# A half unit of w_out products moved inside the fourth visit of each frame

## Chip, cores, metric

The kernel runs on one core of one Trainium2 chip. The metric is device time in microseconds (us) of one execution; three executions of the kernel before took 860.3, 860.36 and 861.01 us, median 860.36.

Engines go by short names: PE is the tensor engine's matmuls, PEld its weight loads, DVE the vector engine, ACT the scalar engine, SP the engine that issues the transfers.

## The reference

An attention over q, k, v (4 batches, 8 heads, 576 positions, 64 wide; four heads see the last 32 positions, four see every 32nd) gives 2304 rows of 512. Two MLPs of the same shape follow, both with weights that come in as inputs:

```
def _moe_ref(x, w_in, w_out):       # x 2304x512, w_in 512x2048, w_out 2048x512
    h = x @ w_in
    r = np.maximum(h, 0.0)
    g = r * r
    return (g @ w_out)

def _moe2_ref(x, w_in, w_out):      # on the result of the first
    h = np.maximum(x @ w_in, 0.0)
    return (h * h @ w_out)
```

## The kernel before

The order of all work is written out by hand (the program is built under a manual schedule), and each engine runs its own instructions in that order. Engines wait for one another by semaphores.

Attention, the first MLP and one narrow block of the second take the first 549 us or so. The rest is the second MLP on four blocks of 512 tokens, and the change lies there. Both products of a block are done by a seven-product scheme (sums and differences of 256-wide quarters, seven products in place of eight). Every operand is split into a high and a low part, so one product is three matmuls: high by high, high by low, low by high.

A block k has eight pairs q of hidden slices. The function `seven` goes over the 32 (k, q) and calls `frame` for all but the last, so 31 times. One call, a frame, does the first product (by w_in) of the next pair and, in between, the second product (by w_out) of this pair:

- The first product is four **visits** (`visit`). The first has 12 matmuls (products "11" and "s2"), the second 6 ("12"), the third 12 ("s1", "s3"), the fourth 12 ("s4", "22"). All four write the same PSUM bank: the pool `ps_h` has one buffer, tile `ps_m`. So the first matmul of each visit waits until the visit before it has been read out.
- The second product is seven **units** of two halves (`n_unit`), 14 half units of 3 matmuls each into other banks (`ps_y`). `seven` deals them into four `gaps`, one behind each visit.

Every one of the 84 matmuls of a frame is 128x128 by 128x256 with a weight load of its own. I call one load with its matmul a **step**. So a frame is, on the tensor engine: first visit 12 steps, `gaps[0]` 9, second visit 6, `gaps[1]` 9, third visit 12, `gaps[2]` 15, fourth visit 12, `gaps[3]` 9.

What the vector engine does around the change, in its order:

```
        add(u..., ps..., u2...)      # reads all of the third visit's bank: u<-ps_m 128x512
        add(a22, ps[:, :HT], u3)     # reads it again: r<-ps_m 128x256
        ...
        each(gaps[2])
        each(late)
        rest(bh[:, 1], bl[:, 1], a22)
        visit(k, q, ps, ("s4", 5), ("22", 6))
        add(of["c"], ps, u)          # reads the fourth visit's bank: c<-ps_m 128x512
```

The fourth visit's first matmul waits for the second of these adds. The next frame's first visit waits for the third, `c<-ps_m`.

In the profile's line numbers of the kernel before, a visit's matmuls are L1279, a half unit's L1306 and the adds L1112. In the first frame of a block (q = 0) the output of the block before is summed and stored as well, so the scalar and vector engines have more to do there. I call the three such frames of which a block precedes (the 9th, 17th and 25th) boundary frames, and the others plain.

Of the kernel before, what the change touches and what calls it, by code (L numbers as in the profile page):

```python
# [169 lines left out]
def tile_attention_then_two_mlps(  # L170
# [218 lines left out]
    def tt(out, in0, in1, op):  # L389
        nc.vector.tensor_tensor(out=out, in0=in0, in1=in1, op=op)  # L390
# [48 lines left out]
    for i in range(0, half2, 2):  # L439
        n = i + 2 if i + 2 < half2 else None  # L440
# [656 lines left out]
    def each(todo):  # L1097
        for one in todo:
            one()

    def high(hi, src):
        nc.scalar.activation(out=hi, in_=src, func=AF.Copy)  # L1102

    def rest(hi, lo, src):
        tt(lo, src, r32(hi), ALU.subtract)
# [5 lines left out]
    def add(dst, src, to, sign=1.0):  # L1111
        nc.vector.scalar_tensor_tensor(  # L1112
            out=dst, in0=src, scalar=sign * W_BACK, in1=to, op0=ALU.mult, op1=ALU.add
        )
# [83 lines left out]
    def x_op(k, i):  # L1198
        at = (k - NB) % 2 * 10 + 2 * i if i < 5 else 10 + 2 * i
        return [  # L1200
            xall[:, 48 + (at + a) * TB:48 + (at + a + 1) * TB].rearrange("p (c n) -> p c n", c=2)
            for a in range(2)
        ]

    def load_x(k, half):
        t0, n = BLOCKS[1][k - NB]
        for c in (2 * half, 2 * half + 1):
            nc.sync.dma_start(out=others[:, c * TB:(c + 1) * TB], in_=y_dram[:, c, t0:t0 + n])
# [30 lines left out]
    pairs7 = [(k, q) for k in range(NB + 1, 2 * NB) for q in range(NF // 2)]  # L1239
# [27 lines left out]
    def m_weights(q, name):  # L1267
        if name[0] == "s":
            return [t[:, int(name[1]) - 1] for t in s_parts[NF + 2 * q]]
        w = wt["in", 1, 2 * q + int(name[0]) - 1]  # L1270
        return [w[:, int(name[1]) - 1, a] for a in range(2)]

    def visit(k, q, ps, *products):
        for half, (name, i) in enumerate(products):
            w_hi, w_lo = m_weights(q, name)
            x_hi, x_lo = x_op(k, i)
            for j in range(2):
                for m, (w, x) in enumerate(((w_hi, x_hi), (w_hi, x_lo), (w_lo, x_hi))):
                    nc.tensor.matmul(  # L1279
                        ps[:, half * HT:(half + 1) * HT],  # L1280
                        lhsT=w[:, j * P:(j + 1) * P],
                        rhs=x[:, j],
                        start=half == 0 and j == 0 and m == 0,
                        stop=half + 1 == len(products) and j == 1 and m == 2,
                    )

    def squares(t):
        nc.vector.scalar_tensor_tensor(out=t, in0=t, scalar=0.0, in1=t, op0=ALU.max, op1=ALU.mult)  # L1288
# [26 lines left out]

        return [lambda t=t: half(t) for t in range(2)]

    def frame(gaps, nxt, cur, copies=((), (), ()), end=False, x=((), (), ()), late=()):

        k, q = nxt  # L1320
        if not of:
            of["r"] = gpool.tile([P, TB], F32, tag="r", name="r", bufs=1)
            of["c"] = gpool.tile([P, TB], F32, tag="sq", name="c", bufs=1)
            shapes = {"bh": ("qk0", 4), "bl": ("qk1", 4), "ah": ("qk2", 3)}
            for t, (tag, n) in shapes.items():
                of[t] = fpool.tile([P, n * HALF], F32R, tag=tag, name=t, bufs=1).rearrange(
                    "p (i n) -> p i n", i=n)
            for t, n in (("al", 2), ("al2", 1)):
                of[t] = gpool.tile([P, 3 * HALF], F32R, tag="gl", name=t, bufs=2)[
                    :, 48:48 + n * HALF].rearrange("p (i n) -> p i n", i=n)  # L1330
        r, c = (of[t].rearrange("p (h n) -> p h n", h=2) for t in ("r", "c"))
        a11, a22, a21, a12 = r[:, 0], r[:, 1], c[:, 0], c[:, 1]
        ah, al, bh, bl = (of[t] for t in ("ah", "al", "bh", "bl"))
        sums_x, high_x, rest_x = x

        def positive(t, src):
            nc.scalar.activation(out=t, in_=src, func=AF.Relu)
            nc.scalar.activation(out=t, in_=t, func=AF.Square)

        if cur:  # L1340
            s13, s24 = (
                gpool.tile([P, TB + P], F32, tag="gh", name="s", bufs=2)[:, :TB].rearrange(
                    "p (i n) -> p i n", i=2)
                for _ in range(2)
            )
            high(ah[:, 2], a12)
            tt(s13[:, 0], a21, a22, ALU.add)
            tt(s13[:, 1], a11, a21, ALU.subtract)
            rest(ah[:, 2], of["al2"][:, 0], a12)
            tt(s24[:, 0], s13[:, 0], a11, ALU.subtract)  # L1350
            tt(s24[:, 1], a12, s24[:, 0], ALU.subtract)
        each(copies[0])
        ps = ps_h.tile([P, TB], F32, tag="h", name="ps_m")
        visit(k, q, ps, ("11", 0), ("s2", 1))
        m, u = (vpool.tile([P, 512], F32, tag="val", name="u") for _ in range(2))

        c11, u2 = m[:, :HT], m[:, HT:]
        u3 = u[:, HT:]
        nc.scalar.activation(out=m, in_=ps, func=AF.Copy, scale=W_BACK)  # L1359
        tt(u2, c11, u2, ALU.add)  # L1360
        each(copies[1])
        if cur:
            high(ah[:, 0:2], s13)
            high(bh[:, 2:4], s24)
        each(copies[2])
        each(gaps[0])
        if end:
            first_sum()
            rest(ah[:, 0:2], al, s13)
        visit(k, q, ps, ("12", 2))  # L1370
        add(c11, ps[:, :HT], c11)
        if cur:
            rest(bh[:, 2:4], bl[:, 2:4], s24)
        if cur and not end:
            rest(ah[:, 0:2], al, s13)
        each(sums_x)
        if end:
            each(high_x)
            each(rest_x)
        positive(a11, c11)  # L1380
        high(bh[:, 0], a11)
        if not end:
            each(high_x)
        each(gaps[1])
        if nxt == pairs7[0]:
            ps = ps_a.tile([P, TB], F32, tag="a", name="ps_m")
        visit(k, q, ps, ("s1", 3), ("s3", 4))
        add(
            u.rearrange("p (h n) -> p h n", h=2),
            ps.rearrange("p (h n) -> p h n", h=2),  # L1390
            u2.unsqueeze(1).to_broadcast([P, 2, HT]),
        )
        add(a22, ps[:, :HT], u3)
        positive(a22, a22)
        high(bh[:, 1], a22)
        rest(bh[:, 0], bl[:, 0], a11)
        if not end:
            each(rest_x)
        each(gaps[2])
        each(late)  # L1400
        rest(bh[:, 1], bl[:, 1], a22)
        visit(k, q, ps, ("s4", 5), ("22", 6))
        add(of["c"], ps, u)
        squares(of["c"])
        each(gaps[3])
# [4 lines left out]
    def first_sum():  # L1410
        acc["p1"] = tile_of("pt")
        nc.scalar.activation(out=acc["p1"], in_=banks["11"], func=AF.Copy, scale=W_BACK)

    def sums_late(last):
        acc["u"], acc["o12"], acc["o"] = tile_of("pt"), tile_of("s"), tile_of("s")
        add(acc["u"], banks["s2t2"], acc["p1"])
        if last:
            add(acc["o12"], banks["s1t1"], acc["u"])
# [99 lines left out]
    def seven():  # L1518
        copies, sums = None, []
        for n, (k, q) in enumerate(pairs7[:-1]):  # L1520
            todo = [one for name in ORDER for one in n_unit(k, q, name)]
            gaps = todo[:3], todo[3:6], todo[6:11], todo[11:]
            end = q == NF // 2 - 1 or n + 2 == len(pairs7)
            more = k < last7
            x = [[], [], []]
            if more and q == 0:
                x_work[k + 1] = x_works(k + 1)
            if more and q > 1:
                x = [list(part) for part in x_work[k + 1][q - 2]]
            late = [lambda: sums_late(not more)] if end else []  # L1530
            if sums:
                first, then = sums.pop(0)
                x[0] += first
                late += then
            frame(gaps, pairs7[n + 1], True, copies or ((), (), ()), end, x, late)
            copies = None
            if more and q in (1, 2):
                load_x(k + 1, q - 1)
            if end and more:
                copies, sums = sums_then(k)  # L1540
        finish()
# [8 lines left out]
    with tc.manual_schedule():  # L1550
# [3 lines left out]
        ps = ps_h.tile([P, TB], F32, tag="h", name="ps_w")[:, :P]  # L1554
# [19 lines left out]
        for s in range(len(steps)):  # L1574
            k, f = steps[s]
            layer, j = blocks[k]
# [41 lines left out]
            if k == NB - 1:  # L1618
                load2("in")
        seven()  # L1620

# [36 lines left out]
```

## Time and profile before

| | us |
|---|---|
| median of three runs | 860.36 (860.3 to 861.01) |
| the profiled execution's own time | 860.37 |
| its span, first to last instruction | 858.6 |
| so around the span | 1.77 |
| PE busy | 847.8 (99%) |
| PEld busy | 770.4 (90%) |
| DVE busy | 681.2 (79%) |
| ACT busy | 526.3 (61%) |

The profile is of one execution. Its own time is within 0.01 us of the median. Busy shares are over all stages. A matmul's busy time is counted from its start to its modelled end, and neighbours overlap, so the distance from one weight load's start to the next says more about pace than the busy time does.

### The profile page before, as it was taken

Reading aid. Unit: us, or ns where it says so; the run is one execution under the profiler, and the core shown is the slowest. Engines: PE = TensorE matmul, PEld = TensorE weight load, DVE = VectorE, ACT = ScalarE, POOL = GpSimd, SP = SyncE. Lnnn points to the kernel's source line nnn. Section 1 sums busy time; section 2 is a strip of 40 time slices with the busy share of each in tenths; the row PEclk is TensorE's granted clock in tenths of the full one; section 3 lists DMA queues with packets and bytes.
Section 4 is the critical chain, followed back from the end, with each engine's and each line's share of the span. In section 5 each row is a group of like instructions: output and inputs, shape, how many; then the busy total and the mean of one; then the engine's idle time right before and its main releaser. Section 6 shows DMA issues by size and latency. Waiting matters only on the chain. (4 is left out here: it accounts for less than half of the span.)

```text
span 858.6 us, 16041 instructions
## 1 busy us (share of the span) xinstructions
PE 847.8 (99%) x5719; PEld 770.4 (90%) x5719; DVE 681.2 (79%) x1710; ACT 526.3 (61%) x1216; POOL 16.8 (2%) x15
## 2 busy tenths in 40 slices
PE   8899999999999999999999999999999999999998
PEld 8778888888788888899888899999999999999998
DVE  5899895489775777478889996678888888888877
ACT  6987775467675666376666774555555564556442
POOL 0610000000000000000000000000000000000000
PEclk9999999999999999999999999999999999999999
DMA  8964721222222221268996476476668667766764
GB/s 268 336 218 160 238 64 45 89 77 76 73 78 97 62 71 59 74 244 296 344 364 211 155 269 233 133 226 202 193 197 282 188 192 238 244 188 197 230 186 133
DMA packets 82399, 155.21 MB, mean 181 GB/s; under 512 B 7568, under 2 KB 36368, under 8 KB 80272
## 3 DMA queue, kind: packets, MB, share of 16 engines
q1 hardware_dynamic: 82320, 154.19, 55.0%
q8 instruction: 45, 0.74, 0.3%
q14 instruction: 34, 0.28, 0.1%
HBM read 127.95 MB, written 26.21 MB: 180 GB/s over the span
## 5 line engine op out<-in xcount | busy, mean ns | idle before, releaser
L975 PE MATMUL ps_h<-xall,w 128*128 128x512 f32 (+1 forms) x1153 | 247.2, 358 | 0.0
L975 PEld LDWEIGHTS ps_h<-xall,w 128*128 128x128 f32 x1153 | 185.1, 188 | 25.9
L975 PE MATMUL ps_y<-gh,w 128*128 128x512 f32 (+1 forms) x640 | 155.8, 374 | 0.7 <-ACT gh L1024 0.7
L975 PEld LDWEIGHTS ps_y<-gh,w 128*128 128x128 f32 x640 | 107.9, 188 | 17.6 <-ACT gh L1024 1.1
L1279 PE MATMUL ps_m<-xall,s 128*128 128x256 f32 x768 | 104.5, 279 | 0.3 <-DVE r L1112 0.3
L1018 ACT ACTIVATE r<-ps_h 128x512 f32<-128x512 f32 x80 | 47.7, 597 | 87.2 <-PE ps_h L975 78.2
L1279 PEld LDWEIGHTS ps_m<-xall,s 128*128 128x128 f32 x768 | 95.5, 188 | 0.9 <-DVE r L1112 0.8
L1306 PE MATMUL ps_y<-w,bh 128*128 128x256 f32 x496 | 91.8, 278 | 0.0
L975 PE MATMUL ps_y<-gl,w 128*128 128x512 f32 (+1 forms) x324 | 83.8, 370 | 0.0
L1279 PE MATMUL ps_m<-xall,w 128*128 128x256 f32 x576 | 83.3, 280 | 0.0
L1306 PEld LDWEIGHTS ps_y<-w,bh 128*128 128x128 f32 x496 | 75.3, 188 | 0.0
L1279 PEld LDWEIGHTS ps_m<-xall,w 128*128 128x128 f32 x576 | 74.2, 188 | 0.4 <-ACT u L1359 0.4
L1029 DVE TENSOR_TENSOR gl<-sq,gh 128x512 fp32r<-128x512 f32 x80 | 55.3, 691 | 21.7 <-ACT gh L1024 17.1
L1306 PE MATMUL ps_y<-w,ah 128*128 128x256 f32 x372 | 70.1, 278 | 0.0
L1306 PE MATMUL ps_y<-w,bl 128*128 128x256 f32 x248 | 68.8, 277 | 0.0
L1027 DVE TENSOR_TENSOR sq<-r 128x512 f32<-128x512 f32 x38 | 26.3, 692 | 50.7 <-ACT r L1018 50.7
L975 PEld LDWEIGHTS ps_y<-gl,w 128*128 128x128 f32 x324 | 55.7, 188 | 9.6 <-DVE gl L1029 0.4
L1306 PEld LDWEIGHTS ps_y<-w,ah 128*128 128x128 f32 x372 | 56.7, 189 | 0.0
L1112 DVE SCALAR_TENSOR_TENSOR u<-ps_m,u 128x256 f32<-128x256 f32 x64 | 35.7, 558 | 25.4 <-PE ps_m L1279 25.3
L680 ACT ACTIVATE s<-s,m 96x128 f32<-96x128 f32 (+2 forms) x88 | 34.3, 390 | 33.6 <-DVE m L564 32.9
L1102 ACT ACTIVATE ah<-c 128x256 fp32r<-128x256 f32 x33 | 13.7, 418 | 63.6 <-DVE c L1288 63.6
L1306 PE MATMUL ps_y<-w,al 128*128 128x256 f32 x186 | 51.7, 278 | 0.0
(121 smaller groups left out, 1500.7 us busy)
## 6 DMA issues: line engine op xcount, KB each, us to landing
w<-w_mem SPq DMA_DIRECT2D x221, 256.0 KB, 2.8
raw<-moe_w_in_d SPq DMA_DIRECT2D x32, 512.0 KB, 5.8
raw<-moe_w_out_d SPq DMA_DIRECT2D x24, 512.0 KB, 5.1
w_mem<-xall SPq DMA_DIRECT2D x16, 512.0 KB, 4.2
w_mem<-xall SPq DMA_DIRECT2D x8, 1024.0 KB, 5.3
xall<-w_mem SPq DMA_DIRECT2D x8, 1024.0 KB, 5.5
qk<-loc_qk_d SPq DMA_DIRECT2D x12, 416.0 KB, 3.1
out_d<-o SPq DMA_DIRECT2D x17, 256.0 KB, 2.4
```

The source lines that it names most:

```text
L680: nc.scalar.activation(out=blk, in_=blk, func=AF.Exp, scale=-1.0, bias=m[:nq, j:j + 1], accum_out=dens[i][:nq, j:j + 1],)
L975: nc.tensor.matmul(y[:, c:c + w], lhsT=lhsT, rhs=rhs[:, c:c + w], start=start and c == 0, stop=stop and c + w == n,)
L1018: nc.scalar.activation(out=r, in_=ps, func=AF.Relu, scale=W_BACK)
L1027: nc.vector.tensor_tensor(out=sq, in0=r, in1=r, op=ALU.mult)
L1029: nc.vector.tensor_tensor(out=lo, in0=sq, in1=r32(h), op=ALU.subtract)
L1102: nc.scalar.activation(out=hi, in_=src, func=AF.Copy)
L1112: nc.vector.scalar_tensor_tensor(out=dst, in0=src, scalar=sign * W_BACK, in1=to, op0=ALU.mult, op1=ALU.add)
L1279: nc.tensor.matmul(ps[:, half * HT:(half + 1) * HT], lhsT=w[:, j * P:(j + 1) * P], rhs=x[:, j], start=half == 0 and j == 0 and m == 0, sto ...
L1306: nc.tensor.matmul(banks[name][:, t * HALF:(t + 1) * HALF], lhsT=g[:, rows], rhs=w, start=first and t == 0 and m == 0, stop=end and t == 1 ...
```

## The change

`visit` gets an argument `between`, work that is issued after its first matmul. `frame` hands one through to its fourth visit. `seven` gives `gaps[2]` four half units in place of five, and the fifth (number 10 of 14, the first half of unit "s3t3") goes in as `between`. The frame that stands in the narrow block calls without it.

```
-    def visit(k, q, ps, *products):
+    def visit(k, q, ps, *products, between=None):
         for half, (name, i) in enumerate(products):
...
                 for m, (w, x) in enumerate(((w_hi, x_hi), (w_hi, x_lo), (w_lo, x_hi))):
+                    if half == 0 and j == 0 and m == 1 and between is not None:
+                        between()
                     nc.tensor.matmul(
...
-        visit(k, q, ps, ("s4", 5), ("22", 6))
+        visit(k, q, ps, ("s4", 5), ("22", 6), between=between)
...
-            gaps = todo[:3], todo[3:6], todo[6:11], todo[11:]
+            gaps = todo[:3], todo[3:6], todo[6:10], todo[11:]
...
-            frame(gaps, pairs7[n + 1], True, copies or ((), (), ()), end, x, late)
+            frame(gaps, pairs7[n + 1], True, copies or ((), (), ()), end, x, late, todo[10])
```

On the tensor engine, from the last but one half unit of `gaps[2]` to the end of the fourth visit of a plain frame, before (`ah` and `al` are the two parts of a hidden operand, `w` the ring of w_out, `xall` and `s` or `w` the visit's operands):

```order
L1306 MATMUL ps_y<-w,ah 128x256 [waits DMAHW2_49]
L1306 MATMUL ps_y<-w,ah 128x256
L1306 MATMUL ps_y<-w,al 128x256 [waits DVE_49]
L1306 MATMUL ps_y<-w,ah 128x256 x2
L1306 MATMUL ps_y<-w,al 128x256
L1306 MATMUL ps_y<-w,ah 128x256 [waits DMAHW3_49]
L1306 MATMUL ps_y<-w,ah 128x256
L1306 MATMUL ps_y<-w,al 128x256
L1279 MATMUL ps_m<-xall,s 128x256 [waits DVE_49]
L1279 MATMUL ps_m<-xall,s 128x256 x5
L1279 MATMUL ps_m<-xall,w 128x256 x6
```

The same place of the changed program:

```order
L1308 MATMUL ps_y<-w,ah 128x256 [waits DMAHW2_49]
L1308 MATMUL ps_y<-w,ah 128x256
L1308 MATMUL ps_y<-w,al 128x256 [waits DVE_49]
L1308 MATMUL ps_y<-w,ah 128x256 x2
L1308 MATMUL ps_y<-w,al 128x256
L1281 MATMUL ps_m<-xall,s 128x256 [waits DVE_49]
L1308 MATMUL ps_y<-w,ah 128x256 [waits DMAHW3_49]
L1308 MATMUL ps_y<-w,ah 128x256
L1308 MATMUL ps_y<-w,al 128x256
L1281 MATMUL ps_m<-xall,s 128x256 x5
L1281 MATMUL ps_m<-xall,w 128x256 x6
```

The visit's first matmul, with its wait for the vector engine, now stands three matmuls earlier, and the half unit with its wait for a transfer stands behind it.

On the same engine in the first boundary frame, around the same place, before:

```order
L1306 MATMUL ps_y<-w,ah 128x256 x2
L1306 MATMUL ps_y<-w,al 128x256
L1306 MATMUL ps_y<-w,ah 128x256 [waits DMAHW0_49,PE_49,Activation_49]
L1306 MATMUL ps_y<-w,ah 128x256
L1306 MATMUL ps_y<-w,al 128x256
L1279 MATMUL ps_m<-xall,s 128x256 [waits DVE_49]
L1279 MATMUL ps_m<-xall,s 128x256 x5
```

And in the changed program:

```order
L1308 MATMUL ps_y<-w,ah 128x256 x2
L1308 MATMUL ps_y<-w,al 128x256
L1281 MATMUL ps_m<-xall,s 128x256 [waits DVE_49]
L1308 MATMUL ps_y<-w,ah 128x256 [waits DMAHW0_49,PE_49,Activation_49]
L1308 MATMUL ps_y<-w,ah 128x256
L1308 MATMUL ps_y<-w,al 128x256
L1281 MATMUL ps_m<-xall,s 128x256 x5
```

There too the same three rows have changed places with the visit's first. All other rows of the tensor engine, and all rows of the other engines and their waits, are the same but for line numbers.

## Rows read from the trace of the kernel before

**Rows 1.** Page, engines: busy us, share of the span, instructions.
```profile
PE 847.8 (99%) x5719; PEld 770.4 (90%) x5719; DVE 681.2 (79%) x1710; ACT 526.3 (61%) x1216; POOL 16.8 (2%) x15
```

**Rows 2.** Windows, one plain and one boundary frame; columns named in the first row.
```profile
core 0: us, PE busy (x) PEld busy (x) DVE busy (x) ACT busy (x) POOL busy (x), PEclk, DMA share, GB/s
646.76:656.49 9.72, 9.72 (x87) 9.72 (x85) 8.29 (x18) 5.20 (x12) 0.00 (x0) 1.00 0.86 293
...
705.09:714.86 9.77, 9.77 (x87) 9.75 (x85) 8.21 (x18) 5.91 (x14) 0.00 (x0) 1.00 0.65 181
```

**Rows 3.** Instructions of tile ps_m from 549 us on: count, ns min/median/max.
```profile
L1112 DVE SCALAR_TENSOR_TENSOR r<-ps_m,u x31: 424/425/425, 553.6 to 845.4; 128x256 f32<-128x256 f32 x31
```

**Rows 4.** Timeline, weight loads, plain frame: start us, length of the run, instruction.
```profile
646.76 0.78 PEld L1279 LDWEIGHTS ps_m<-xall,w 128*128 128x128 f32 x6
...
648.53 1.45 PEld L1279 LDWEIGHTS ps_m<-xall,s 128*128 128x128 f32 x12
649.91 0.30 PEld L1306 LDWEIGHTS ps_y<-w,bh 128*128 128x128 f32 x2
...
651.27 0.30 PEld L1306 LDWEIGHTS ps_y<-w,ah 128*128 128x128 f32 x2
...
651.61 0.78 PEld L1279 LDWEIGHTS ps_m<-xall,s 128*128 128x128 f32 x6
...
653.02 0.31 PEld L1306 LDWEIGHTS ps_y<-w,ah 128*128 128x128 f32 x2
...
654.09 0.77 PEld L1279 LDWEIGHTS ps_m<-xall,w 128*128 128x128 f32 x6
...
656.49 0.19 PEld L1279 LDWEIGHTS ps_m<-xall,w 128*128 128x128 f32 x1
```

**Rows 5.** Timeline, DVE, same plain frame.
```profile
650.22 0.69 DVE L1112 SCALAR_TENSOR_TENSOR u<-ps_m,u 128x512 f32<-128x512 f32 x1 [0.21 <-PE ps_m L1279]
650.95 0.42 DVE L1112 SCALAR_TENSOR_TENSOR r<-ps_m,u 128x256 f32<-128x256 f32 x1
...
653.34 0.69 DVE L1112 SCALAR_TENSOR_TENSOR c<-ps_m,u 128x512 f32<-128x512 f32 x1 [0.15 <-PE ps_m L1279]
```

**Rows 6.** Timeline, weight loads, the second boundary frame.
```profile
710.03 0.77 PEld L1279 LDWEIGHTS ps_m<-xall,s 128*128 128x128 f32 x6
...
711.41 0.30 PEld L1306 LDWEIGHTS ps_y<-w,ah 128*128 128x128 f32 x2
...
712.47 0.30 PEld L1279 LDWEIGHTS ps_m<-xall,w 128*128 128x128 f32 x2
```

**Rows 7.** Timeline, DVE, the second boundary frame.
```profile
709.55 0.42 DVE L1112 SCALAR_TENSOR_TENSOR r<-ps_m,u 128x256 f32<-128x256 f32 x1
...
711.72 0.69 DVE L1112 SCALAR_TENSOR_TENSOR c<-ps_m,u 128x512 f32<-128x512 f32 x1
```

**Rows 8.** Timeline, weight loads, the first boundary frame.
```profile
632.18 0.77 PEld L1279 LDWEIGHTS ps_m<-xall,s 128*128 128x128 f32 x6
...
633.59 0.31 PEld L1306 LDWEIGHTS ps_y<-w,ah 128*128 128x128 f32 x2
...
634.65 0.30 PEld L1279 LDWEIGHTS ps_m<-xall,w 128*128 128x128 f32 x2
```

**Rows 9.** Timeline, weight loads, the third boundary frame.
```profile
787.84 0.77 PEld L1279 LDWEIGHTS ps_m<-xall,s 128*128 128x128 f32 x6
...
789.22 0.30 PEld L1306 LDWEIGHTS ps_y<-w,ah 128*128 128x128 f32 x2
...
790.27 0.30 PEld L1279 LDWEIGHTS ps_m<-xall,w 128*128 128x128 f32 x2
```

**Rows 10.** Timeline, weight loads, the last frame.
```profile
846.11 0.77 PEld L1279 LDWEIGHTS ps_m<-xall,s 128*128 128x128 f32 x6
...
847.52 0.31 PEld L1306 LDWEIGHTS ps_y<-w,ah 128*128 128x128 f32 x2
```

More of the change, by code (lines that the diff above doesn't have):

```diff
@@ L1316, in n_unit, with frame @@
         return [lambda t=t: half(t) for t in range(2)]
-    def frame(gaps, nxt, cur, copies=((), (), ()), end=False, x=((), (), ()), late=()):
+    def frame(gaps, nxt, cur, copies=((), (), ()), end=False, x=((), (), ()), late=(),
+              between=None):
         k, q = nxt
```

## The prediction

> **What bounds the kernel now.** I read the page's engine lines first. PE is busy 99% of the span and its loads 90% [rows 1], which says only that the tensor engine hardly pauses. Then I asked for windows of single frames. A plain frame takes 9.72 us with the clock granted at 1.00, its upper level of 2.4 GHz; a boundary frame 9.77 us, at the same clock [rows 2]. The vector engine is busy 8.29 us of those 9.72, so it is not the bound on average, but it has little to give away.
>
> An average can't tell what a wait is worth, so the third view is the timeline of one plain frame, weight loads first. Reading start to start, with the steps of each stretch counted from the code, `gaps[2]` runs 15 steps from 649.91 to 651.61, that is 113 ns a step. The fourth visit runs 12 steps from 651.61 to 653.02, 117.5 ns a step [rows 4]. So the engine never stands still here, and it has two paces at one clock, about 113.3 and 117.5 ns. `gaps[3]` takes 1.07 us for 9 steps, 653.02 to 654.09, and there something else comes in, as the next part shows.
>
> Last, the vector engine over the same stretch. It starts on the third visit's bank at 650.22, released by PE with 0.21 us of idle time before; so it was waiting, and its work there follows the last matmul of the third visit. Its second add on that bank is 650.95 to 651.37 [rows 5]. There are 31 such adds, one a frame, all 424 or 425 ns long [rows 3]. The fourth visit's first load comes at 651.61, 0.24 us later. That 0.24 us is all the slack that the fourth visit's wait has. A second margin lies behind: the add of the fourth visit's bank is 653.34 to 654.03, and the next first visit's load comes at 654.09, 0.06 us after. That is the distance at which a load follows when it has in fact been waiting: in the second boundary frame the add ends at 709.55 + 0.42 = 709.97 and the load starts at 710.03 [rows 6, 7]. So the next first visit is already released by the vector engine, and `gaps[3]` just covers that wait.
>
> **What the change costs, step by step.** It adds and removes no instruction. Nothing on DVE, ACT or SP moves, nor does a transfer: the moved half is a first half, and ring loads are issued behind second halves. It takes three steps from ahead of a wait and puts them behind it.
>
> 1. *The wait.* In the plain frame the fifth half unit starts at 651.27. The visit's first load would now want that place. The bank is free at 651.37, and the load follows an add by 0.06 us, so it starts at 651.43. PE stands for 0.16 us. Behind it in PE's order stand the moved half, the other 11 matmuls of the visit and `gaps[3]`; DVE's add of the fourth visit's bank and ACT's and DVE's work on the hidden operands wait for these.
>
> 2. *From there to the end of the visit* are now 15 steps. How fast they run after a stop is not shown for exactly this order. The nearest rows are the three boundary frames, where the fourth visit already starts late: 12 steps take 710.03 to 711.41 = 1.38, 632.18 to 633.59 = 1.41, 787.84 to 789.22 = 1.38 us [rows 6, 8, 9], mean 1.39, 116 ns a step. I take that: 15 steps, 1.74 us. The bounds are the two paces, 1.70 and 1.76 us. `gaps[3]` starts at 653.17 in place of 653.02.
>
> 3. *`gaps[3]` to the next first visit* is the wait for the add, not a matter of pace: 1.06, 1.06 and 1.05 us in the boundary frames, 1.07 in the plain one; in the second boundary frame the add ends at 711.72 + 0.69 = 712.41, again 0.06 us ahead of the load [rows 6, 7]. 653.17 + 1.06 = 654.23, against 654.09. A plain frame gets 0.14 us longer; with the bounds, 1.70 + 1.05 gives 0.09 and 1.76 + 1.07 gives 0.17. Nothing later in the frame takes this back: the loads run through to the next frame at 656.49, so a late first visit is a late everything.
>
> 4. *Boundary frames.* There the bank comes free so late that the visit starts at 710.03 whatever stands ahead of it. Before, all five halves were done by then; now four are and PE waits the longer. 710.03 + 1.74 + 1.06 = 712.83 against 712.47: 0.36 us. By the same sum the others give 0.33 and 0.37; together 1.06, bounds 0.91 and 1.15.
>
> 5. *The last frame* has no first visit behind it; PE runs on to the end. It pays the stop alone, 0.16 us, at the pace that it has (12 steps from 846.11 to 847.52, 117.5 ns [rows 10]). If the stop left PE at the quick pace for the 69 steps to the end, 69 x 4.2 ns = 0.29 us would come back, and the term is -0.13.
>
> Sum: 27 x 0.14 + 1.06 + 0.16 = 5.0 us, counting the first frame as plain. With the quick pace 27 x 0.09 + 0.91 - 0.13 = 3.2, with the slow 27 x 0.17 + 1.15 + 0.16 = 5.9. The profiled execution took 860.37 us, the median of the runs to 0.01, so the sum can be set on it: **865.4 us**, by its own bounds 863.6 to 866.3.
>
> One rule of the Trainium skill bears on step 1. In the trace the load, not only the matmul, begins after the add: 709.97 to 710.03 [rows 6, 7]. The page "TensorE: Matmul & The Clock Gate", section "Step-by-step: what each phase is for", says that the engine's queue may pull a weight load ahead of matmuls in flight while matmuls keep program order. By its second half the moved steps can't pass the waiting one, as in my sum; by its first half the waiting load could be done in the shadow of the wait. The rows above don't show that, and I keep it as the second rival.
>
> **The rivals.**
>
> *Quick pace throughout (not slower).* The paces change only near the start of a visit: in the plain frame the second visit and `gaps[1]` run 15 steps in 646.76 to 648.53, 118 ns, the third visit 12 steps in 1.38, 115 [rows 4]. The change adds a stop and one more switch between the two kinds of matmul, and either might tip PE into the quick pace for good. In `gaps[2]` it holds that for 15 steps. Then steps 2 and 5 go to their lower bounds, and the second visit with `gaps[1]` gives 1.77 - 1.70 = 0.07 us a frame. A plain frame costs 0.02, a boundary frame 0.23 to 0.25, and the last frame gives 0.20: 0.54 + 0.70 - 0.20 = 1.0 us, 861.4. It decides from the point where 15 steps of the second visit and its gap take 1.70. Against it: the boundary frames had a stop and yet averaged 116 ns behind it.
>
> *The load hides in the wait.* If the load is done by the time that the bank comes free, the matmul starts one load earlier, and a load is at most a step, 0.11 us. 31 x 0.11 = 3.4 us less: 862.0. All boundary frames speak against it.
>
> *Slow pace throughout.* If the extra switch leaves PE at 117.5 ns in the first visit and `gaps[0]` (21 steps, now 654.09 to 656.49 = 2.40, then 2.47) and in the third visit (1.38, then 1.41), a plain frame costs 0.17 + 0.10 = 0.27. 27 x 0.27 + 1.15 + 0.30 + 0.26 = 9.0 us, 869.4. Against it: a first visit that has waited for DVE runs quick now.
>
> **How the numbers follow.** About 0.2%, 1.7 us, is what runs of this kernel can tell from no change. The forecast has 0.80, since the stop is forced by rows and only the pace is open; quick throughout 0.09, the hidden load 0.05, slow throughout 0.06. To be faster by 0.2% the first two rivals would have to come together (861.4 - 3.4 = 858.0): 0.04, out of their 0.14. The remaining 0.10 of them lies within 0.2% or close to it: same 0.10. Slower is 0.86. The range 862.4 to 867.2 holds the forecast with its bounds and about a microsecond on either side, for a wait in the boundary frames or a first frame that differs from what I read; it leaves out the three rivals, 0.20.
>
> **What would show it.** Right: the fourth visit's first load 0.05 to 0.06 us after the end of the add `r<-ps_m` in every plain frame (0.24 now), and 0.27 to 0.28 us after the load ahead of it in place of 0.11; a plain frame of 9.81 to 9.89 us; boundary frames some 0.35 longer; the add `c<-ps_m` still ending 0.06 ahead of the first visit's load; DVE's and ACT's durations unchanged. Wrong: a first load sooner than 0.05 us after the add, so that the order of waits isn't what I took it for; 15 steps of the second visit and `gaps[1]` in 1.70 us (quick throughout); or a first visit with `gaps[0]` above 2.45 us (slow throughout). What I don't know is what makes the two paces; that is where the size can go astray, and with it the sign only if both favourable rivals hold.

## The result

The changed kernel takes 865.7 us (median of 4 runs, 865.47 to 866.73) against 860.33 us before: ratio 1.0056, 95% interval 1.0042 to 1.0069. Here and below the ratio is an estimate over all runs and not the quotient of the two medians, which is 1.0062 here and lies inside the interval. It is slower by 5.4 us. Forecast were 865.4 us, in a range of 862.4 to 867.2.

The profiled execution has a span of 864.1 us against 858.6, 5.5 us more. The page's engine line of the changed kernel, to be held beside [rows 1]:

```profile
PE 853.4 (99%) x5719; PEld 772.9 (89%) x5719; DVE 681.1 (79%) x1710; ACT 526.0 (61%) x1216; POOL 17.7 (2%) x15
```

Instruction counts are the same, and DVE and ACT are as busy as before. PE's busy time grew by 5.6 us with no matmul more; the ends of matmuls are modelled, so that line can't tell a stop from work. The page's group of the third and fourth visits' loads shows a part of it in its idle time, which rose from 0.9 to 4.2 us. First the kernel before, then the changed one (count, busy us, mean ns, idle us before, releaser and its part):

```profile
L1279 PEld LDWEIGHTS ps_m<-xall,s 128*128 128x128 f32 x768 | 95.5, 188 | 0.9 <-DVE r L1112 0.8
L1281 PEld LDWEIGHTS ps_m<-xall,s 128*128 128x128 f32 x768 | 97.8, 188 | 4.2 <-DVE r L1112 1.8
```

The releaser named, for 1.8 of the 4.2 us, is the add `r<-ps_m`, the one that the prediction spoke of; for the rest the page names none. The two windows, a plain and a boundary frame, that answer to [rows 2]:

```profile
core 0: us, PE busy (x) PEld busy (x) DVE busy (x) ACT busy (x) POOL busy (x), PEclk, DMA share, GB/s
639.00:648.86 9.86, 9.86 (x87) 9.78 (x86) 8.90 (x19) 4.57 (x11) 0.00 (x0) 1.00 0.69 214
708.08:718.21 10.13, 9.97 (x87) 9.77 (x86) 8.29 (x18) 5.91 (x14) 0.00 (x0) 1.00 0.63 189
```

A plain frame is 0.14 us longer, the boundary frame 0.36, both with the clock granted at 1.00. Weight loads of that plain frame, in order of time, against [rows 4]:

```profile
639.00 0.78 PEld L1281 LDWEIGHTS ps_m<-xall,w 128*128 128x128 f32 x6
...
640.77 1.45 PEld L1281 LDWEIGHTS ps_m<-xall,s 128*128 128x128 f32 x12
642.15 0.30 PEld L1308 LDWEIGHTS ps_y<-w,bh 128*128 128x128 f32 x2
...
643.40 0.19 PEld L1308 LDWEIGHTS ps_y<-w,al 128*128 128x128 f32 x1
643.66 0.19 PEld L1281 LDWEIGHTS ps_m<-xall,s 128*128 128x128 f32 x1
643.77 0.31 PEld L1308 LDWEIGHTS ps_y<-w,ah 128*128 128x128 f32 x2
...
644.13 0.66 PEld L1281 LDWEIGHTS ps_m<-xall,s 128*128 128x128 f32 x5
644.71 0.76 PEld L1281 LDWEIGHTS ps_m<-xall,w 128*128 128x128 f32 x6
645.39 0.30 PEld L1308 LDWEIGHTS ps_y<-w,ah 128*128 128x128 f32 x2
...
646.45 0.77 PEld L1281 LDWEIGHTS ps_m<-xall,w 128*128 128x128 f32 x6
...
648.86 0.19 PEld L1281 LDWEIGHTS ps_m<-xall,w 128*128 128x128 f32 x1
```

And the vector engine of the same frame, against [rows 5]:

```profile
642.46 0.69 DVE L1112 SCALAR_TENSOR_TENSOR u<-ps_m,u 128x512 f32<-128x512 f32 x1 [0.21 <-PE ps_m L1281]
643.18 0.42 DVE L1112 SCALAR_TENSOR_TENSOR r<-ps_m,u 128x256 f32<-128x256 f32 x1
...
645.71 0.69 DVE L1112 SCALAR_TENSOR_TENSOR c<-ps_m,u 128x512 f32<-128x512 f32 x1
```

The add on the third visit's bank ends at 643.60, and the fourth visit's first load comes at 643.66, 0.06 us after it and 0.26 after the load ahead of it, where 0.11 is usual. The moved half unit's own wait, for a transfer, adds nothing: its first load comes 0.11 us behind the visit's, at 643.77. From the visit's first load on, 15 steps take 1.73 us, to 645.39. The add of the fourth visit's bank ends at 646.40, and the next first visit begins at 646.45.

In the trace 31 frames, from the load at 549.48 to that at 851.06, took 301.59 us before, and 306.66 us (549.91 to 856.57) now: 5.08 us more. The other 0.43 us of the span lies ahead of the first changed frame, which begins that much later.

### The profile page after: what moved, and what is told of

It reads as the page before. It is cut to its first block, busy times and chain, and to the rows that moved or that the text cites. A ratio compares the mean times of both kernels' runs of the same rounds, so it can differ in the third digit from the quotient of the medians.

```text
span 864.1 us, 16041 instructions
## 1 busy us (share of the span) xinstructions
PE 853.4 (99%) x5719; PEld 772.9 (89%) x5719; DVE 681.1 (79%) x1710; ACT 526.0 (61%) x1216; POOL 17.7 (2%) x15
## 4 chain that ended last, share of the span: by engine, by line
PE 93%; DVE 4%; ACT 2%; issue 0%; DMA 0%; DVEq 0%; ACTq 0%
PE ps_h L975 24%; PE ps_y L975 22%; PE ps_m L1281 18%; PE ps_y L1308 16%; PE ps_y L1145 2%; PE ps_s L632 2%; PE ps_pt L764 2%; PE ps_x L708 2%; PE ps_o L780 2%; PE ps_s L534 1%; DMA y_dram<-o 0%; PE ps_w L1559 0%; PE ps_x L826 0%; DVE o L1112 0%; ACT others L1433 0%
## 5 line engine op out<-in xcount | busy, mean ns | idle before, releaser
L1281 PE MATMUL ps_m<-xall,s 128*128 128x256 f32 x768 | 112.3, 282 | 0.7 <-DVE r L1112 0.7
L1281 PEld LDWEIGHTS ps_m<-xall,s 128*128 128x128 f32 x768 | 97.8, 188 | 4.2 <-DVE r L1112 1.8
```

The source lines that it names most:

```text
L1281: nc.tensor.matmul(ps[:, half * HT:(half + 1) * HT], lhsT=w[:, j * P:(j + 1) * P], rhs=x[:, j], start=half == 0 and j == 0 and m == 0, sto ...
```

## The experiments

Two theories stood against each other. A is the prediction's: the fourth visit's first load stops until the vector engine has left the bank, and what stands behind it is three steps longer. B: the cost is the additional change between the two kinds of matmul inside the visit, wherever the wait falls. A run's total also holds the stages ahead, which begin or end up to 1.8 us apart between profiled executions of these kernels, so beside each median I give the time of the 31 frames in that run's trace (301.59 us before, 306.66 us with the change). The ratios are to the kernel before on the same chip, which ran at 860.79 us beside the first four experiments and at 860.68 beside the last two. In the result above it ran at 860.33.

**The change, with the bank free sooner.** The second add takes the first add's result from SBUF in place of the bank. The kernel computes other values there; the vector engine's work is the same in number and size.

```
-        add(a22, ps[:, :HT], u3)
+        add(a22, u[:, :HT], u3)
```

> The changed kernel, with the second add on the third visit's bank reading the first add's result instead of the bank (so this kernel computes other values there); the vector engine has as many instructions of the same size, but the bank is free after the first add, about 0.45 us sooner. Theory A (the cost is the stop at the fourth visit's first load, which waits for that second add, and the three steps behind it): the stop of 0.15 us is gone, the visit's first load stands at 4.51 us of a plain frame in place of 4.66, 15 steps and 1.06 us later the next first visit starts at about 7.31 against 7.32 in the kernel before, so the frames are 9.70 to 9.76 us and the whole run 860 to 861 us. Theory B (the cost is the additional change between visit and half unit inside the fourth visit, whatever the wait): 865 to 866 us as the changed kernel.

It took 861.32 us (10 runs), ratio 1.0001, interval 0.9992 to 1.0011, 0.3 us above A's range; 31 frames 302.32 us. The vector engine and the loads of a plain frame:

```profile
670.49 0.69 DVE L1112 SCALAR_TENSOR_TENSOR u<-ps_m,u 128x512 f32<-128x512 f32 x1 [0.21 <-PE ps_m L1281]
671.22 0.43 DVE L1112 SCALAR_TENSOR_TENSOR r<-u 128x256 f32<-128x256 f32 x1
...
671.43 0.19 PEld L1308 LDWEIGHTS ps_y<-w,al 128*128 128x128 f32 x1
671.54 0.19 PEld L1281 LDWEIGHTS ps_m<-xall,s 128*128 128x128 f32 x1
671.66 0.30 PEld L1308 LDWEIGHTS ps_y<-w,ah 128*128 128x128 f32 x2
...
673.30 0.31 PEld L1308 LDWEIGHTS ps_y<-w,ah 128*128 128x128 f32 x2
...
674.36 0.77 PEld L1281 LDWEIGHTS ps_m<-xall,w 128*128 128x128 f32 x6
```

The bank is free at 671.18. The visit's first load, at 671.54, follows the one ahead of it by 0.11 us. The half unit still stands inside the visit, so the additional change of kind is there, and nearly the whole cost is gone: 0.73 us is left of 5.08 in the frames, 0.33 of it in a single frame that is longer than its neighbours. In that frame the scalar engine waited long for a transfer of the next block's operands, and the vector engine's later work, the add `c<-ps_m` included, came late behind it:

```profile
661.62 0.63 ACT L1102 ACTIVATE xall<-others 128x512 fp32r<-128x512 f32 x1 [1.78 <-DMA others<-y_dram]
```

The longest such wait was 1.5 us in the kernel before. Plain frames are 9.73 us. The 15 steps took 1.76 us, the slow pace. B as the account of the cost falls: at most the 0.4 us left beside that frame can be its part.

**Control: the kernel before, with the same edit.**

> The kernel before with the same edit to the second add (other values there too), as the control for the run of the changed kernel with that edit. Theory A: the plain frames had no stop, so they stay at 9.72 us; only the three boundary frames lose their late start of about 0.09 us each; 860.0 to 860.4 us. Theory B: the same.

It took 861.3 us (10 runs), ratio 1.0005, interval 0.9996 to 1.0015; 31 frames 301.53 us, against 301.59 without the edit. The total lies above the range forecast, as did 860.79 us of the kernel before beside it. The boundary frames lost less than A said, 0.05, 0.02 and 0.01 us in place of 0.09: the pace behind the late start had been quicker in two of them, and in all three the next first visit, still released by the add `c<-ps_m`, now comes 1.10 us after the start of `gaps[3]`, where it was 1.06. So the edit in itself gives nothing, and the run above reads as it stands.

**The stop without the half unit inside.**

```
-            gaps = todo[:3], todo[3:6], todo[6:11], todo[11:]
+            gaps = todo[:3], todo[3:6], todo[6:10], todo[10:]
```

> Four half units ahead of the fourth visit, none inside, four behind it. Theory A: the stop of 0.15 us at the visit's first load stays; the next first visit is then no longer released by the add but comes when the 12 steps of the visit and the 12 behind it are through, 4.66 + 1.39 + 1.36 to 1.41 = 7.41 to 7.46 us into a plain frame against 7.32; plain frames 9.81 to 9.86 us, the run 864 to 866 us, about as the changed kernel. Theory B (the additional change between visit and half unit costs): with none inside, 860 to 861 us.

It took 866.83 us (4 runs), ratio 1.0065, interval 1.0049 to 1.0081; 31 frames 306.98 us. The total came near A's range, 0.8 us above it, but the way there was another:

```profile
670.08 0.77 PEld L1279 LDWEIGHTS ps_m<-xall,w 128*128 128x128 f32 x6
...
674.50 0.19 PEld L1306 LDWEIGHTS ps_y<-w,al 128*128 128x128 f32 x1
674.73 0.77 PEld L1279 LDWEIGHTS ps_m<-xall,s 128*128 128x128 f32 x6
...
677.47 0.78 PEld L1279 LDWEIGHTS ps_m<-xall,w 128*128 128x128 f32 x6
...
679.94 0.19 PEld L1279 LDWEIGHTS ps_m<-xall,w 128*128 128x128 f32 x1
```

The visit's first load comes 0.23 us behind the load ahead of it, a stop of about 0.12 us where A had 0.15. The frame begins at 670.08 and takes 9.86 us, most others 9.87, where A had 9.81 to 9.86. The next first visit starts 7.39 us into it, not 7.41 to 7.46: the 24 steps from the fourth visit on ran in 2.74 us, 114 ns each. That is 0.07 us later than before. The other half of the frame's 0.15 us comes from the first visit and `gaps[0]`, which now take 2.47 us for 21 steps (118 ns) where they took 2.40 [rows 4]. With no half unit inside the visit the cost is as large as with it, which again speaks against B; but only half of it has arisen when the next first visit starts, and the other half is a change of pace behind it that A didn't have.

**The half unit behind the sixth product in place of the first.**

```
-                    if half == 0 and j == 0 and m == 1 and between is not None:
+                    if half == 1 and j == 0 and m == 0 and between is not None:
```

> The half unit stands inside the fourth visit behind its sixth product in place of its first. Theory A: the same stop, the same number of steps between it and the add of the visit's bank: plain frames 9.84 to 9.89 us, 865 to 866.5 us. Theory B in its narrower form (a single product followed at once by a half unit costs): less, 861 to 864 us.

It took 867.16 us (4 runs), ratio 1.0068, interval 1.0046 to 1.0089, 0.7 us above A's range; 31 frames 307.57 us. A plain frame (columns as in the windows above), and from one frame of 10.45 us, some 0.6 us over its neighbours, the scalar engine's wait and the next first visit's load:

```profile
669.41:679.28 9.87, 9.87 (x87) 9.79 (x86) 8.28 (x18) 5.20 (x12) 0.00 (x0) 1.00 0.61 189
...
734.06 0.63 ACT L1102 ACTIVATE xall<-others 128x512 fp32r<-128x512 f32 x1 [2.24 <-DMA others<-y_dram]
...
737.01 0.19 PEld L1281 LDWEIGHTS ps_m<-xall,w 128*128 128x128 f32 x1 [0.51 <-DVE c L1112]
```

The long frame is again one in which the scalar engine waited for a transfer, here 2.24 us, and the add `c<-ps_m` came late. Why the transfer landed late stays open. Most plain frames are 9.87 us against 9.85 in the changed kernel. Where the half unit stands inside the visit hardly matters, and B's narrower form falls too.

**Two half units inside**, in 27 of the 31 frames (the four that end a block keep the changed kernel's order).

```
+            at = 10 if end else 9
-            gaps = todo[:3], todo[3:6], todo[6:10], todo[11:]
+            gaps = todo[:3], todo[3:6], todo[6:at], todo[11:]
...
-            frame(gaps, pairs7[n + 1], True, copies or ((), (), ()), end, x, late, todo[10])
+            frame(gaps, pairs7[n + 1], True, copies or ((), (), ()), end, x, late,
+                  lambda: each(todo[at:11]))
```

> Three half units ahead of the fourth visit and two behind its first product, in 27 of the 31 frames; in the four frames that end a block one inside, as in the changed kernel. Theory A: the bank comes free at the same time, so each further half unit costs its three steps in full, 0.35 us: the stop in a plain frame is 0.15 + 0.34 = 0.49 us and the next first visit starts at 4.66 + 18 x 0.116 + 1.06 = 7.81 us against 7.32. 24 x 0.49 + 3 x 0.71 + 4 x 0.2 = 14.7, so 875 us (873.5 to 876). Theory B (the additional change between visit and half unit costs, and there are as many of them as in the changed kernel): 865 to 867 us.

It took 875.65 us (4 runs), ratio 1.0171, interval 1.0156 to 1.0186; 31 frames 316.40 us. The loads of a plain frame:

```profile
676.38 0.19 PEld L1308 LDWEIGHTS ps_y<-w,al 128*128 128x128 f32 x1
676.99 0.19 PEld L1281 LDWEIGHTS ps_m<-xall,s 128*128 128x128 f32 x1 [0.42 <-DVE r L1112]
...
680.13 0.65 PEld L1281 LDWEIGHTS ps_m<-xall,w 128*128 128x128 f32 x5
```

The load comes 0.61 us after the one ahead of it, a stop of 0.50 us, and the trace now names the add as its releaser. Most plain frames take 10.20 us, 0.35 longer than with one half unit inside. Each further half costs its three steps in full, as A says of a bank that comes free at a fixed time.

**No stop at the fourth visit, but a half unit from behind it inside.** Five halves stay ahead; `between` is half number 11 (like the change's number 10, counted from 0), and two are left in `gaps[3]`.

```
-            gaps = todo[:3], todo[3:6], todo[6:10], todo[11:]
+            gaps = todo[:3], todo[3:6], todo[6:11], todo[12:]
...
-            frame(gaps, pairs7[n + 1], True, copies or ((), (), ()), end, x, late, todo[10])
+            frame(gaps, pairs7[n + 1], True, copies or ((), (), ()), end, x, late, todo[11])
```

> Five half units stay ahead of the fourth visit as in the kernel before; the half unit behind its first product is taken from the three that stood behind the visit, so two are left there. Theory A: no stop at the fourth visit, but the visit's last matmul comes three steps later and the add of its bank releases the next first visit 1.06 us after that, so the engine stops there for about 0.35 us: plain frames 9.72 + 0.32 = 10.04 us, the run 869 to 871 us. Theory B: as the changed kernel, 865 to 866 us. Theory C (only waits at the fourth visit matter, and the space behind it has slack): 860 to 861 us.

It took 871.32 us (4 runs), ratio 1.0117, interval 1.0100 to 1.0134, 0.3 us above A's range; 31 frames 312.27 us. Loads of a plain frame:

```profile
675.84 0.19 PEld L1308 LDWEIGHTS ps_y<-w,al 128*128 128x128 f32 x1
675.96 0.19 PEld L1281 LDWEIGHTS ps_m<-xall,s 128*128 128x128 f32 x1
...
678.31 0.19 PEld L1308 LDWEIGHTS ps_y<-w,bl 128*128 128x128 f32 x1
678.78 0.30 PEld L1281 LDWEIGHTS ps_m<-xall,w 128*128 128x128 f32 x2 [0.28 <-DVE c L1112]
```

The fourth visit is on time (0.12 us behind the load ahead), and the next first visit stops instead, 0.47 us behind the load ahead of it, released by the add `c<-ps_m`. This shows the second margin of the prediction: `gaps[3]` had nothing to spare, so three steps more inside the visit go through to the next frame, here 0.33 to 0.35 us in most frames, where 0.32 was expected. B and C fall.

## Why the prediction was right, point by point

*The wait (step 1).* Right to 0.01 us: 0.16 forecast in a plain frame, 0.15 measured (0.26 from load to load, less 0.11). The prediction calls the 0.24 us from add to load all the slack; a waiting load follows by 0.06 of it, so the margin was 0.18, and with that step 1 in fact reckons. Freeing the bank sooner takes it away, a second half unit lengthens it by that half's own length. The load begins at least 0.05 us after the add in every frame, so the second rival, a load done in the shadow of the wait, did not happen. That bears on the page "TensorE: Matmul & The Clock Gate" of the Trainium skill, section "Step-by-step: what each phase is for": loads may be pulled ahead of matmuls in flight, but no run here shows one pulled ahead of the wait that it carries.

*15 steps at 116 ns, then 1.06 us (steps 2 and 3).* Right: 1.73 us (forecast 1.74, bounds 1.70 and 1.76), then 1.06. Most plain frames run 9.85 us, some 9.84, 9.87 or 9.89, by the pace that the steps behind the stop take. The steps that make up the pace, slow first and quick later (4 steps from 643.66 in 0.47 us, the 6 from 644.71 in 0.68), were not predicted, only their mean.

*Boundary frames (step 4).* Forecast +0.33, +0.36 and +0.37, measured 10.08, 10.13 and 10.12 us against 9.81, 9.77 and 9.77: +0.28, +0.36 and +0.35.

*The last frame (step 5).* +0.11 in place of 0.16, between its bounds of -0.13 and 0.16; part of the slow pace was given back.

*What was missed.* The frames that end a block (the 8th, 16th, 24th) were counted as plain. They cost 0.29, 0.23 and 0.23 us. Their fourth visit's first matmul waits for two engines, DVE and ACT, and its load comes 0.12 us after the add, not 0.06, though ACT was not late: its last instruction ahead of that load had ended at 622.57. The 8th frame:

```profile
622.15 0.42 ACT L1102 ACTIVATE bh<-r 128x256 fp32r<-128x256 f32 x1
...
623.09 0.42 DVE L1112 SCALAR_TENSOR_TENSOR r<-ps_m,u 128x256 f32<-128x256 f32 x1
...
623.63 0.19 PEld L1281 LDWEIGHTS ps_m<-xall,s 128*128 128x128 f32 x1
```

Before, the 0.24 us between add and load had covered this. In the 8th frame the first visit with `gaps[0]` also ran slow. The 31 frames add up to 5.08 us where the sum said 5.0, and that closeness is partly luck: the block ends gave 0.32 us more than they were counted for, and the plain frames (0.13), the boundary frames (0.07) and the last frame (0.05) together 0.25 less. The 0.43 us that the changed kernel's profiled execution lost ahead of the frames is no part of the prediction.

*The rivals.* Neither "quick throughout" nor "slow throughout" came: in nearly all frames the second visit with `gaps[1]` takes 1.77 us (639.00 to 640.77), as before, and the first visit with `gaps[0]` 2.41 us (646.45 to 648.86) against 2.40. Around the first boundary single stretches turned, 2.47 us in the 8th frame and 1.72 in the 9th. The price of "quick throughout" in a boundary frame was 0.21 to 0.25 us by the prediction's own terms, not 0.23 to 0.25; its total of 0.70 is right.

## What to carry to other kernels

A wait in the middle of a busy engine's order has a margin that the timeline shows: the end of the releaser against the start of the waiter, less the distance at which a waiter follows when it is in fact late (0.06 us here, 0.12 with two semaphores). In these runs work moved from ahead of such a wait to behind it stopped the engine for its length less that margin (0.34 less 0.18 us for the first half unit) and, once the margin was used up, for its whole length (0.35 us for the second). As the next wait down the chain had no margin either, nearly all of the stop went through to the next frame. Before moving work into the middle of a product that another engine reads, look what waits for that product's end: here `gaps[3]` had no slack, and a half unit taken from there into the visit cost its whole length, 0.33 to 0.35 us, though the visit itself started on time.

## What the runs showed of the hardware that was not expected

With the clock granted at 1.00 throughout, a step of 128x128 weights and 256 columns has two paces, 113 and 117.5 to 118 ns. In these traces PE keeps one over many steps and goes over to the other within the first steps of a visit or, behind a stop, some four to ten steps on. In the plain frame of [rows 4], for example, the first three steps of the third visit take 117 to 122 ns each and the other nine 113 or 114. In the kernel before, the second and fourth visits with their gaps ran slow and the first and third quick. With the stop alone the pattern was the other way round: the fourth visit with what stands behind it quick (114 ns), the first with `gaps[0]` slow (2.47 us in place of 2.40), the second with `gaps[1]` quick (1.72 in place of 1.77), the third slow (1.41 in place of 1.38). Behind a stop of the changed kernel the quick pace came back in most frames, but in a few, such as the 4th and the 19th, all 15 steps ran slow (1.76 us). What sets the pace stays open: the additional change of kind inside the visit didn't turn it in the run with the bank freed sooner (15 steps in 1.76 us), and no run here varied the pace alone.
